# Even-odd token order kept to the store, 64-row tiles for the pair units and low-rank products, and totals moved by small transfers, in a fused recurrence and MLP kernel

## The chip, the cores and the metric

The kernel runs on one core of a Trainium2 chip. The metric is device time in microseconds (us). Three timed runs of the kernel before gave 163.08, 163.26 and 163.46 us, a median of 163.26. One further execution was profiled. The engines are TensorE (PE: matrix products, with PEld its weight loads), VectorE (DVE), ScalarE (ACT), GpSimd (POOL), and SyncE (SP), whose queue issues most transfers.

## What is computed

A gated linear recurrence on 4 batches, 8 heads, 768 tokens and head size 48, and then a mixer with a low-rank product over tokens and an MLP over channels:

```
for t in range(S):
    state = alpha[:, :, t, :, None] * state + einsum('bhd,bhe->bhde', k[:, :, t], v[:, :, t])
    y[:, :, t] = einsum('bhd,bhde->bhe', q[:, :, t], state)
x  = y with its heads side by side           # 4 x 768 x 384
h  = xt @ U @ V                              # xt: x transposed; U is 768 x 32, V is 32 x 768
u  = x + h transposed
out = u + maximum(u @ w_ch1, 0) @ w_ch2      # 384 -> 1536 -> 384
```

## The kernel before

**Chunks and pair units.** Each batch is cut into six chunks of 128 tokens. Inside a chunk the recurrence is a masked product: with cumulative sums of log(alpha) from a triangular product (lines 415 to 417 and 590), the kernel forms `rk = k * exp(-sum)` and `rq = q * exp(sum)`, transposes both (459, 632), takes scores (486, 653), masks them on DVE into `pm` (497, 663), and adds what the state brings in (560, 710) to the masked scores times v (567, 712). The state for the next chunk is the state product of rk and v (518, 676) plus the old state, scaled by the chunk's total decay `tot`.

Batches 2 and 3 go chunk by chunk (`stage_gla`). Batches 0 and 1 are "paired" (`stage_pair`): a unit holds 256 tokens of four heads, and a partition holds two neighbouring tokens, so that each row of a load is twice as long. Partitions 0 to 63 belong to the unit's first chunk, 64 to 127 to its second. To keep the two chunks apart, v is written into a tile `rw` with zeros where the other chunk's columns are, so one product of all 128 rows serves both. The transposed q is put back into natural token order when it is copied out of PSUM, which is a strided copy; from there on x is in natural order.

**Mixer.** `stage_mix` multiplies x by U in 32-column tiles of PE (line 727), which leaves four partial sums below one another; V is held four times below itself in `vm_sb`, so that the next product adds the four. Batch 0 builds the transposed u directly (746, 749). Batches 1 to 3 make u per chunk by a 128-row product with `vm_sb` (758) and an addition on DVE (759), and transpose it (774). Then come the first MLP product (801) with its Relu (811 on ACT, 813 on DVE), the second (831), a final addition (843) and the store of 128 rows (848) through SP.

**Order.** Every step is an entry of a plan. A fixed text, `TABLE`, lists all entries in one order, with a letter where an engine is chosen (A is ACT, V is DVE, G is POOL), and `Plan.run` issues them in it. So the order on every engine is written out, and buffers (36 `io` tiles for loads, 8 PSUM banks) are assigned by the plan's own estimates. Filler products that compute nothing (line 317) stand in the first 28 us. The loads wait on SP in the order of the table; SP also waits there for buffers to come free. In batch 3 the transposes of rk and rq are transfers issued by ACT (623), not PE products.

The totals of `stage_gla` come from four one-column products per chunk (592), then two exponentials on ACT (605):

```
nc.scalar.activation(tot()[:, i : 2 * HP : 2, 0], cb()[:, DM : DM + HP], AF.Exp, bias=offb[:, i : i + 1])
```

Of the kernel before, what the change touches and what calls it, by code (L numbers as in the profile page):

```python
# [159 lines left out]
69 65 61 201 157 179 63 64 62 160 204 162 165V 73 66 67 71 77 159A 161 164G 158G 167 182 169V 184 163 206 183 207 224 205 75 166 173 70 168V 186V 174  # L160
187V 170 227 229 175 188 209V 189 68 191A 232G 228 247 171 211 190V 176 172 192 194 234 250 78 208G 230 213A 180A 251 236A 185 210 181G 212V 195 177 81
214 254G 193 178V 3 256 268 252 253 196 215 74 271 72 79 197 76 4 231G 82 83 80 273 199 233 203A 202G 235A 84 198 258V 216 217 255G 272 218 226G 219
274 225A 237 85 93 6 257 5 259A 222 220 240 25 29 27 89 15 17 13 19 23 21 87 33 94 35 86 31 238 239 200A 275G 223A 95 90 221 241 260 276V 242 277 249G
248G 279A 278 2 270G 243 245 261 263 244 262 47 92 280A 264 91 97 37 43 269A 281 265 284 39 41 51 49 101 88 45 285 266 96 0 1 8 30G 28G 283 282 286 388
246A 432 391 435 267V 287 298 18G 11 9 16G 14G 288V 394 7A 289 105 57 59 53 55 290 438 437 436 10A 12V 102 291A 100 103 20G 295 292 304 301 98 293 294V
24G 22G 307 296 299 302 308 297V 305 26A 410 99 306V 303V 413 300A 326 322 107 309A 350 336 416 393 392 337V 310 414 396G 334 324 325A 415 311V 327V
335V 351V 323V 34G 32G 104 106 109 108 110 344 342 320 340 346 338 318 321A 36A 343V 395V 319A 314 398 330 341A 345A 315A 339V 439V 417V 400V 440G 356
354 412G 117 111 357V 355V 397 352 441 328 331A 347A 443V 419 442 316 411A 418G 353V 329V 444V 420 332 455 399A 333A 317A 426 348 312 421V 422V 40A
349A 38G 44G 42G 427 458 313V 428 423 429G 390G 46G 401 445 460 459 461 48A 52A 425 446 424 402 368 358 363 433G 434G 389G 50A 478 430 481 482 483 484
54G 60G 58A 499 369 447 431V 403 373 359 404 364 448 405 406 407V 449 450V 485V 408 502 56A 503 456A 409V 486V 365 370 451 371 487 462G 463V 488 504  # L170
457A 507G 360 471 489A 490A 505 465 467A 464 361 366 479A 480A 113 367 119 118 466V 472 374 491 473G 506G 468 492 375 509 494 453 469 470 511A 112 508
474 452G 378 495 618 475G 620 476 510A 376 501A 496G 621 454V 512 493 500G 515 624G 379 514 497 516 517G 513 626 623 657 622 625V 477A 129 362 114 115
659 518 662 498A 519A 627 380 629A 520 521A 637 660 628V 630 381 632 383 661 663G 664G 619G 522 524 133 121 523 525 530 384 536 534 528 531 529 537 535
526 385 527A 532 116 120 124 125 127 141 123 122 134 533V 126 665 131 372 137 135 639 666 668V 633 538 539V 634 640 641 540 642 562 548 558 542 541A
563V 643G 644G 572 646 549V 559V 717 648V 631 667V 573A 645 544 582 556 677 647A 545A 557A 649 832 669 130 128 386 583V 671 566 568 670 651 650 554 719
546 584 567A 543A 721 720 555V 697 658A 585V 586 679 547V 587V 569V 578 681 722 638G 834 652 574 635 653 575V 836 835 680 636A 682 837 387 153 655 560
550 580 684V 656V 654V 552 699 683G 553V 551A 867 701 838G 704G 570 686 685 564 579V 581V 571V 565V 702 700 678A 561A 672 703V 687V 724V 593 588 706
705 692 594 595 673 598 589 675 145 132 674V 693 707V 596 708V 839V 676V 840 688A 849 709 689 711 710 691 690 723G 851 599 725 727A 576 698G 726 600
590 712 854 577A 869 841 728A 852 718A 591 694V 872 870 613 614 729 713 731 730 138 149 382 377 143 136 142 885 921 853 871 714G 147 139 615 603 887
715 732 695 601 716V 696V 604 842 733A 889 734 923 608 735A 855G 874G 616 844 843 738 748 873G 833G 744 903 888 925 924 926 742 609 749 743 745 602 592  # L180
140 146 155 154 750 751 739 892G 610 736 746 605 752 737 850G 890 875 876 747V 753V 740 845 847 905 846 794 796 741V 797V 606 856G 891G 927G 778 768
774 848A 857 611 795V 894 858 908 893 906 760 780 764 862 152 150 144 761V 148 151 612 156 617 775V 781V 765V 863 769V 788 782 800 790 798 784 791V
779V 785V 772 758 759V 789A 907 799A 773A 801A 754 755V 756 757V 877 859 895 860 861 878 896 904A 783A 776 762 928G 864G 807 770 766 929 930 868G 909G
886G 910G 763V 767V 771V 911 802 865 912 880 803 916 808 897 777V 881 882G 879 809 898 804 812 883 813 899 900V 810 805 931 913 917 932 884A 866A 914
933 915 918G 786 792 901 827 811 806 922G 793A 902A 787A 822 934 919 920A 823 824 935V 936 828 937A 829 938 940 946 825 939 947 941 817 814 944 826 597
607 945 818 942 948 949V 943A 950 819 820 951 956 966 968 952 830 953 815 962 974 954 960 975V 970 963V 955V 976 982 994 969V 961V 995V 971A 967V 1000
992 988 993A 977A 957A 978 986 964 987V 1001V 980 958 989V 981V 959A 984 1002 990 996 983A 965A 1003A 985V 991V 997A 998 999A 972 1014 1024 1015 1004
1025 1026 1019 1020 1027 979V 973V 1021 1005 1009 1010 831 816 1028 1022 1006 1016 1007 1011 1023 821 1008 1017 1029 1012 1030 1032 1018 1013 1031 1033
1034
# [3 lines left out]
def mm(*cols):  # L193
    return sum(max(c / 2.4 + 2.5, 25.0) for c in cols)
# [3 lines left out]
def kernel(  # L198
# [12 lines left out]
    nc = tc.nc  # L211
# [20 lines left out]
    TRD = {(3, c) for c in range(NC)}  # L232
# [5 lines left out]
    u_in = const.tile([128, NC, R], FP32, name="u_in")  # L238
    v_in = const.tile([R, S], FP32, name="v_in")
# [9 lines left out]
    mask2 = const.tile([C, 2, 2 * C], BF16, name="mask2")  # L249
    for x in (filler, tri, ident, mask2, blocks):  # L250
# [6 lines left out]
        out=mask2, in_=mask2, compare_op=ALU.is_gt, fill=1.0, base=0, pattern=[[1, 2], [-1, 2 * C]], channel_multiplier=2  # L257
# [26 lines left out]
    nc.vector.tensor_copy(maskp[0:64, 0], mask2[0:64, :, 0:C])  # L284
    nc.vector.tensor_copy(maskp[64:128, 0], mask2[64:128, :, C : 2 * C])
    rv2_s = slots("rw", 4, [C, 2, HP, 2, D], BF16)
    for x in rv2_s:
        nc.vector.memset(x, 0.0)
    maskc = const.tile([C, 1, C], BF16, name="maskc")
    P.add({"POOL": 250}, lambda e: nc.gpsimd.tensor_copy(maskc[:, 0, :], ut_ones), w=["maskc"])  # L290
    sel = const.tile([R, 4, R], BF16, name="sel")
# [8 lines left out]
    tots = Pool(slots("tot", 4, [128, HP * 2, 1], FP32))  # L300
    qts = Pool(slots("qt", 4, [128, HP, C], BF16))
# [31 lines left out]
    def small():  # L333
        P.add({"SP": 450.0}, lambda e: nc.sync.dma_start(u_in, moe_U.rearrange("(c p) r -> p c r", p=128)), w=["u_in"])
        P.add({"SP": 500.0}, lambda e: nc.sync.dma_start(v_in, moe_V), w=["v_in"])
        P.add({"POOL": 300, "ACT": 280}, lambda e: copy(e, u_sb, u_in), r=["u_in"], w=["u"])
        P.add({"POOL": 800}, lambda e: nc.gpsimd.tensor_copy(v_bf, v_in), r=["v_in"], w=["v_bf"])
        for i in range(2):
            vb = Buf(bank)
            sl = slice(i * TW, (i + 1) * TW)  # L340
            P.add({"PE": mm(TW)}, lambda e, vb=vb, sl=sl: nc.tensor.matmul(vb()[:, 0:TW], lhsT=sel.rearrange("r a b -> r (a b)"), rhs=v_bf[:, sl], start=True, stop=True), r=["v_bf"] + [("sel", g) for g in range(4)], w=[vb], mode="V")
            P.add({"DVE": 470, "ACT": 390}, lambda e, vb=vb, sl=sl: copy(e, vm_sb[:, sl], vb()[:, 0:TW]), r=[vb], w=[("vm", i)])

    def weight(dst, src, key, engs):
        t = Buf(io)
        P.add({"SP": 590.0}, lambda e: nc.sync.dma_start(flat(t), src), w=[t])
        P.add(engs, lambda e: copy(e, dst, flat(t)), r=[t], w=[key])
# [4 lines left out]
    def weights1():  # L352
        for g in range(4):
            cs = slice(g * DM, (g + 1) * DM)
            for ct in range(NCT):
                weight(w1_sb[:, ct, cs], moe_w_ch1[ct * 128 : (ct + 1) * 128, cs], ("w1", g, ct), {"POOL": 485, "ACT": 435})

    def weights2():
        for jt in range(NJ):
            weight(w2_sb[:, jt, :], moe_w_ch2[jt * 128 : (jt + 1) * 128, :], ("w2", jt), {"POOL": 485, "ACT": 435})  # L360
# [24 lines left out]
    def xk(b, xb, c):  # L385
        return [(xb, c, 0), (xb, c, 1)] if b in PAIR else [(xb, c)]

    def stage_pair(b, u, sprev, xb):
# [12 lines left out]
        rv = Buf(rv2s)  # L401
# [5 lines left out]
        for c in range(2):  # L407
            P.add({"POOL": 480, "ACT": 420}, lambda e, c=c: f_rv(e, c), r=[vt], w=[(rv, c)])
# [494 lines left out]
```

## Time and profile before

| | |
|---|---|
| median of three runs | 163.26 us |
| profiled execution, whole | 164.47 us |
| its span | 162.7 us |
| PE, DVE, ACT, POOL busy | 95%, 77%, 52%, 35% |
| mean granted PE clock | 0.998 |
| transfers | 30.37 MB, mean 187 GB/s |

The span is what the profiler saw, from the first instruction to the last; the whole adds what lies around it. Busy shares are means over stages. PE's products are pipelined: the duration shown for one is its latency, and consecutive ones start closer together than that. In a merged timeline row, `x8` after a form says that eight such products follow each other, and the second number is the time from the first's start to the last's end. DMA in the slices is the mean busy share of 16 transfer engines.

### The profile page before, as it was taken

The page shows a single profiled execution, that of the slowest core. Times are in us where ns is not written, and L with a number is a line of the kernel's source. Part 1 is how long each engine was busy: PE and PEld are TensorE (multiplying, and loading weights), DVE is VectorE, ACT ScalarE, POOL GpSimd, SP SyncE. Part 2 cuts the span into 40 slices and gives each one's busy share as a digit, 9 for nine tenths or more (in the row PEclk, how much of TensorE's full clock was granted, in tenths as well). Part 3 has the DMA queues.
Part 4 walks back from the last instruction along what each step waited for, and adds up shares of the span by engine and source line. Part 5 has one row for each costly group of instructions (what it writes and reads, how often), then busy time and mean ns, then how long its engine had stood idle before and what let it go on. Part 6 is the DMA issues. An engine that isn't in the chain of part 4 may idle for free.

```text
span 162.7 us, 4458 instructions
## 1 busy us (share of the span) xinstructions
PE 154.3 (95%) x1683; PEld 102.4 (63%) x1683; DVE 125.8 (77%) x274; ACT 85.4 (52%) x218; POOL 57.7 (35%) x92
## 2 busy tenths in 40 slices
PE   7789999999999899999999999999899999999993
PEld 2356787667776676766666666766466656666662
DVE  6478996689969996979999888988978557961441
ACT  5479899557885778468982386307102411153000
POOL 3037985756264172550092056634413000000000
PEclk9999999999999999999999999999999999999999
DMA  5999999999999998998997898989982040200134
GB/s 124 271 279 302 250 277 285 326 316 330 355 253 248 207 209 185 186 202 168 216 246 64 198 204 209 218 135 189 218 108 99 0 144 7 97 0 4 48 145 145
DMA packets 89701, 30.37 MB, mean 187 GB/s; under 512 B 83376, under 2 KB 89648, under 8 KB 89680
## 3 DMA queue, kind: packets, MB, share of 16 engines
q1 hardware_dynamic: 83152, 28.52, 71.1%
q10 hardware_dynamic: 6528, 1.57, 7.4%
q8 instruction: 13, 0.21, 0.6%
q14 instruction: 8, 0.07, 0.1%
HBM read 23.79 MB, written 4.72 MB: 175 GB/s over the span
## 4 chain that ended last, share of the span: by engine, by line
PE 84%; DVE 6%; ACT 3%; DMA 3%; issue 1%; SPq 1%; DVEq 0%; ACTq 0%
PE ps L801 29%; PE ps L831 27%; PE ps L459 3%; DMA io<-in_alpha_dram 3%; PE ps L653 2%; PE ps L567 2%; PE ps L774 2%; DVE rq L446 2%; PE ps L486 2%; PE ps L758 2%; PE ps L632 2%; PE ps L518 1%; PE ps L712 1%; PE ps L590 1%; DVE st L531 1%
## 5 line engine op out<-in xcount | busy, mean ns | idle before, releaser
L831 PE MATMUL ps<-w_sb,h1t 128*128 128x384 bf16 (+2 forms) x300 | 53.1, 319 | 0.0
L801 PE MATMUL ps<-uT,w_sb 128*128 128x384 bf16 x288 | 50.9, 326 | 0.0
L801 PEld LDWEIGHTS <-w_sb 128*128 128x128 bf16 x288 | 26.8, 98 | 16.2 <-DVE uT L326 0.2
L831 PEld LDWEIGHTS <-h1t 128*128 128x128 bf16 x300 | 27.2, 98 | 15.2 <-issue 0.3
L813 DVE TENSOR_SCALAR h1t<-ps 128x384 bf16<-128x384 f32 x59 | 30.0, 551 | 6.4 <-PE ps L801 6.3
L811 ACT ACTIVATE h1t<-ps 128x384 bf16<-128x384 f32 x37 | 16.8, 500 | 16.7 <-PE ps L801 16.5
L843 DVE TENSOR_TENSOR ou<-ub,ps 128x384 f32<-128x384 bf16 (+2 forms) x19 | 9.9, 529 | 10.5 <-PE ps L831 10.3
L612 POOL TENSOR_TENSOR rk<-io,ai 128x384 bf16<-128x384 f32 x11 | 10.7, 977 | 16.7 <-ACT ai L600 11.2
L497 DVE TENSOR_TENSOR pm<-ps,maskp 128x512 bf16<-128x512 f32 x24 | 15.7, 684 | 0.3 <-PE ps L486 0.2
L663 DVE TENSOR_TENSOR pm<-ps,maskc 128x512 bf16<-128x512 f32 x24 | 15.2, 684 | 0.7 <-PE ps L653 0.6
L324 ACT CAST xb<-ps 128x384 bf16<-128x384 f32 x13 | 5.9, 480 | 14.2 <-PE ps L712 14.2
L759 DVE TENSOR_TENSOR ub<-xb,ps 128x384 bf16<-128x384 bf16 x18 | 9.0, 550 | 2.5 <-PE ps L758 2.5
L687 POOL TENSOR_TENSOR st<-sm,tot 128x384 bf16<-128x384 f32 x4 | 3.3, 828 | 18.6 <-DVE sm L699 18.6
L328 POOL CAST w_sb<-io 128x384 bf16<-128x384 f32 x16 | 7.9, 505 | 5.4 <-DMA io<-in_moe_w_ch_dram 5.2
L446 POOL TENSOR_TENSOR rk<-io,ai 128x384 bf16<-128x384 f32 x7 | 6.4, 912 | 9.1 <-ACT ai L431 6.3
L324 ACT COPY qt<-ps 128x512 bf16<-128x512 bf16 x11 | 7.7, 700 | 3.2 <-PE ps L459 1.9
L612 POOL TENSOR_TENSOR rq<-io,aa 128x384 bf16<-128x384 f32 x8 | 7.3, 914 | 2.7 <-issue 1.6
L400 ACT ACTIVATE lt<-io 128x384 bf16<-128x384 f32 x12 | 6.3, 530 | 2.9 <-DMA io<-in_alpha_dram 2.9
L317 PE MATMUL ps<-filler 128*128 128x512 bf16 x17 | 6.5, 510 | 1.2 <-DVE filler L251 1.2
L326 DVE CAST xb<-ps 128x384 bf16<-128x384 f32 x11 | 6.1, 554 | 1.8 <-PE ps L712 1.5
L446 POOL TENSOR_TENSOR rq<-io,aa 128x384 bf16<-128x384 f32 x6 | 5.9, 981 | 4.2 <-ACT aa L432 3.9
L605 ACT ACTIVATE tot<-ps,offb 128x4 f32<-128x4 f32 x24 | 4.9, 274 | 4.7 <-PE ps L801 4.5
(124 smaller groups left out, 266.2 us busy)
## 6 DMA issues: line engine op xcount, KB each, us to landing
io<-in_alpha_dram SPq DMA_DIRECT2D x24, 192.0 KB, 4.1
io<-in_q_dram SPq DMA_DIRECT2D x24, 192.0 KB, 4.3
io<-in_v_dram SPq DMA_DIRECT2D x24, 192.0 KB, 4.1
io<-in_k_dram SPq DMA_DIRECT2D x24, 192.0 KB, 4.2
io<-in_moe_w_ch_dram SPq DMA_DIRECT2D x24, 192.0 KB, 4.4
out_dram<-ou SPq DMA_DIRECT2D x23, 192.0 KB, 2.3
out_dram<-ou SPq DMA_DIRECT2D x1, 128.0 KB, 1.7
v_in<-in_moe_V_dram SPq DMA_DIRECT2D x1, 96.0 KB, 3.5
```

Of the source, the lines that this page charges most:

```text
L324: nc.scalar.copy(dst, src)
L328: nc.gpsimd.tensor_copy(dst, src)
L446: eng.tensor_tensor(jh(dst()[:, :, 0:D]), raw(a), jh(x()), op=ALU.mult)
L497: nc.vector.tensor_tensor(dst, s2, maskp.to_broadcast([C, 2, 2, C]), op=ALU.mult)
L612: eng.tensor_tensor(dst()[:, :, 0:D], a(), x(), op=ALU.mult)
L663: nc.vector.tensor_tensor(pm()[:, :, par, :], s2, maskc.to_broadcast([C, HP, C]), op=ALU.mult)
L759: P.add({"DVE": 465}, lambda e, c=c, hb=hb: nc.vector.tensor_tensor(ub()[:, c, :], xb()[:, c, :], hb()[:, 0:DM], op=ALU.add), r=[hb] + xk( ...
L801: nc.tensor.matmul(hb()[:, 0:TW], lhsT=w1_sb[:, ct, jt * 128 : (jt + 1) * 128], rhs=uT()[:, ct, tt * TW : (tt + 1) * TW], start=(ct == 0), ...
L811: nc.scalar.activation(dst, hb()[:, 0:TW], AF.Relu)
L813: nc.vector.tensor_scalar_max(dst, hb()[:, 0:TW], 0.0)
L831: nc.tensor.matmul(hb()[:, 0 : hi - lo], lhsT=h1()[:, jt, c * C : (c + 1) * C], rhs=w2_sb[:, jt, lo:hi], start=(jt == 0), stop=(jt == NJ - ...
L843: nc.vector.tensor_tensor(ou()[:, lo:hi], base()[:, c, lo:hi], hb()[:, 0 : hi - lo], op=ALU.add)
```

## The change

1. **Token order.** In batches 0 and 1 x stays in the order in which the loads bring it: in each chunk first the 64 even tokens, then the 64 odd. The transposes of q are written so that its copy out of PSUM is plain. U and V get copies in that order (`up_sb`, `vp_sb`) for batches 0 and 1, and `u_sb`, `vm_sb` are made from them by a product with a permutation and by two copies on POOL. The output rows of a chunk go out in two transfers of 64 rows.
2. **Pair units in 64-row tiles** (`HALF`). v is cast once into a plain tile. The state products and the products of masked scores with v are issued per chunk on 64 rows of PE, into two PSUM banks; two such products can be in PE at once. The part from the state is issued after them, untiled, and the output leaves in two copies of 192 columns instead of one of 384.
3. **Low-rank products in 64-row tiles** (`ROWS`, batches 1 to 3). The U products are made twice, so that each half of the 128 rows holds the whole sum; then two chunks' low-rank products run on the two halves.
4. **Late totals** (`TOTD`, batches 2 and 3). The one-column products go. ACT takes the exponential of the last 32 rows of the sums, and two transfers of 48 pieces of 16 bytes move the last row into `tot`, for five of six chunks; the sixth needs none.
5. **Engines and order.** v and weight casts may go to DVE, and `TABLE` is another order throughout, which begins with a load of q, then three of alpha.

New lines: state products 570, output products in the chunk 617, from the state 629, permutation 360, U products 869, low-rank 903, totals 705 and 708, stores in halves 1009. Cut to its core:

```diff
+        for j in range(2):
+            P.add({"SP": 330.0}, lambda e, j=j: nc.sync.dma_start(u_in[64 * j : 64 * j + 64], moe_U.rearrange("(c m j) r -> j m c r", c=NC, j=2)[j]), w=[("u_in", j)])
...
-        for c in range(2):
-            P.add({"POOL": 480, "ACT": 420}, lambda e, c=c: f_rv(e, c), r=[vt], w=[(rv, c)])
+        if apart:
+            P.add({"POOL": 480, "ACT": 420, "DVE": 340}, lambda e: copy(e, flat(rv), flat(vt)), r=[vt], w=[(rv, 0), (rv, 1)], port=True)
...
+                if apart:
+                    for c in range(nch):
+                        r = slice(64 * c, 64 * c + 64)
+                        for m in parts:
+                            nc.tensor.matmul(
+                                db[c]()[m, a * 2 * D : (a + 1) * 2 * D],
+                                lhsT=rk()[r, HP * j + 2 * a : HP * j + 2 * a + 2, :].rearrange("t h w -> t (h w)")[:, m],
+                                rhs=raw(rv)[r, j, 2 * a : 2 * a + 2, :],
+                                start=(n == 0), stop=(n == 3 and not onpe), skip_group_check=True,
+                            )
+                    continue
...
+            def f_yn(e):
+                for h in range(HP):
+                    for j in range(2):
+                        for c in range(2):
+                            r = slice(64 * c, 64 * c + 64)
+                            for m in parts:
+                                nc.tensor.matmul(
+                                    yb[c]()[m, h * D : (h + 1) * D], lhsT=pm()[r, (h // 2) * 2 + j, h % 2, m], rhs=raw(rv)[r, j, h, :],
+                                    start=(h == 0 and j == 0), stop=(before[c] is None and h == HP - 1 and j == 1), skip_group_check=True,
+                                )
...
+        def f_end(e):
+            nc.scalar.activation(end()[C - 32 : C].rearrange("t i d p -> t p i d"), cb()[C - 32 : C, 0:DM].rearrange("t (p i d) -> t p i d", i=2, d=D), AF.Exp)
+
+        def f_move(e, i):
+            nc.sync.dma_start(tot()[64 * i : 64 * i + D, HP * i : HP * i + HP, 0], end()[C - 1 : C, i].rearrange("t d p -> t (d p)"))
...
+                for gg in (g % 2, g % 2 + 2) if twice else (g,):
+                    nc.tensor.matmul(
+                        xu()[32 * gg : 32 * gg + R, 0:DM], lhsT=us[:, c, :], rhs=xb()[:, c, :],
+                        start=(c < (2 if twice else 4)), stop=(c + (2 if twice else 4) >= NC), skip_group_check=True,
+                    )
...
+        def f_low(e, c):
+            for i in range(2):
+                r = slice(64 * i, 64 * i + 64)
+                nc.tensor.matmul(hbs[c + i]()[:, 0:DM], lhsT=vs[r, (c + i) * C : (c + i + 1) * C], rhs=utx()[r], start=True, stop=True)
...
+                def f_store(e, z=z):
+                    nc.sync.dma_start(out[b, c * C : (c + 1) * C, :].rearrange("(m j) x -> j m x", j=2)[z], ou()[64 * z : 64 * z + 64, :])
```

## The prediction

> **What bounds the kernel now.** I read the page's busy shares and its 40 slices first, then the list of waits of TensorE (PE), then the PE groups by form, then PE's timeline where small products meet long ones, then the landings of the transfers.
>
> ```profile
> span 162.7 us, 4458 instructions
> PE 154.3 (95%) x1683; PEld 102.4 (63%) x1683; DVE 125.8 (77%) x274; ACT 85.4 (52%) x218; POOL 57.7 (35%) x92
> PE   7789999999999899999999999999899999999993
> DVE  6478996689969996979999888988978557961441
> PEclk9999999999999999999999999999999999999999
> DMA  5999999999999998998997898989982040200134
> ```
> PE is busy in nearly every slice at full granted clock. VectorE (DVE) runs at 0.9 in the first stage and in the middle; the DMA engines are full until slice 30 (about 120 us).
>
> ```profile
> PE ps L459 <- DVE rq L446: 1.2, 2, 0.9
> PE ps L653 <- DVE pm L663: 0.8, 1, 0.8
> 115.77 0.23 PEld L653 LDWEIGHTS <-kt 48*128 48x128 bf16 x8 [0.96 <-DMA kt<-rk]
> ```
> Waits of PE, and a weight-load row. Comparing each start with the one before, I find 2.4 us of PE stall from 28.5 us to the end, nearly all in two places: 1.1 at 52.3 us, behind a run of DVE work, and 1.0 at 115 us, where weights wait for a transposing transfer. Before 28.5 us, from the first real product (6.65 us) on, there are about 3 us of gaps. So the time is PE's work plus a few waits, and the first term is a count.
>
> ```profile
> L567 PE MATMUL ps<-rw,pm 128*128 128x96 bf16 x96 | 6.0, 206 | 0.0
> L758 PE MATMUL ps<-utx,vm_sb 128*128 128x384 bf16 x18 | 4.4, 326 | 0.0
> L518 PE MATMUL ps<-rw,rk 128*128 128x192 bf16 x32 | 4.0, 246 | 0.4 <-ACT rw L324 0.4
> L592 PE MATMUL ps<-ones,lt 128*128 128x1 bf16 x48 | 2.9, 164 | 0.0
> L727 PE MATMUL ps<-xb,u_sb 128*32 128x384 bf16 x24 | 2.0, 333 | 0.0
> L518 PE MATMUL ps<-rw,rk 128*128 128x96 bf16 x16 | 1.4, 207 | 0.0
> ```
> The groups that the change replaces. The mean is a latency; what counts is the step from start to start:
>
> ```profile
> 64.33 0.40 PE L653 MATMUL ps<-qt,kt 48*128 48x128 bf16 x8
> 64.66 0.82 PE L831 MATMUL ps<-w_sb,h1t 128*128 128x384 bf16 x4
> 65.32 0.65 PE L758 MATMUL ps<-utx,vm_sb 128*128 128x384 bf16 x3
> 79.99 0.36 PE L712 MATMUL ps<-rv,pm 128*128 128x48 bf16 x8
> 80.20 0.33 PE L710 MATMUL ps<-st,qt 128*128 128x96 bf16 x4
> 80.36 0.36 PE L712 MATMUL ps<-rv,pm 128*128 128x48 bf16 x8
> ```
> Four of 384 columns take 0.66 us (64.66 to 65.32): 162 ns each. Eight of 48 columns take 0.21 (25 ns each), four of 96 take 0.16 (42 each). L653 has pairs in 64-row tiles: single starts in the trace are 3 to 4 ns apart inside a pair, for the weight loads too, and 56 from pair to pair, so two 128-column products cost what one does. Going into and out of a tiled shape costs 95 ns each time (L831 to L653: 258 ns instead of 162; L653 back: 148 instead of 56).
>
> **PE's work, part by part.** Removed: totals of batches 2 and 3 (L592), 48 x 25 = 1.20 us. State products (L518), 32 x 82 + 16 x 42 = 3.30. Output products in the chunk (L567), 96 x 42.5 = 4.08. Low-rank products (L758), 18 x 162 = 2.92. U products (L727), four batches of two rounds of 162 = 1.30. Sum 12.80.
>
> Added: state products in 64-row tiles, 32 pairs and 16 singles of 96 columns, 48 x 42 = 2.02. Output products, 192 of 48 columns in 96 pairs: no row shows a pair that short. Two ends: 25 ns for a pair, as for one product in L712 (2.40 us), or 50, if two short ones follow each other (4.80). I take 25, since L653's loads and products start together, and in 16 products of 64x64 tiles (L486) a product starts every 14 ns. Low-rank in pairs, 9 x 162 = 1.46. U products twice over in batches 1 to 3, 2 + 9 rounds = 1.79. The reordering of U, 0.08. Sum 7.75. Net -5.05.
>
> Against it stand changes of tile shape. In PE's order there are 39 before and 73 after (state and output products now are tiled and lie between untiled ones): 34 x 0.095 = +3.23. **PE's work: -1.8 us.**
>
> Here a rule weighs against the change. The Trainium skill, TensorEngine Tiling (Array Packing), section Instruction Overhead, says that each matmul carries about 60 cycles, and warns not to split by tiling when a dimension is already short. Taken per instruction (25 ns at 2.4 GHz), the 192 output products would cost an estimated 4.8 us and PE's work would grow by 0.6 us. The 14 ns steps of L486 contradict that reading across tiles; no row here shows it at 48 columns.
>
> **First stage (to the first MLP product, 28.92 us).** The first load issued is now a q; the first PE step needs the second load, not the third. These landed at 4.0 and 6.05 us, so PE starts up to 2 us earlier. Later the stage is held by DVE and ScalarE (ACT). Per pair unit the change removes one of two v casts of 0.5 us (ACT or POOL), makes the q eviction plain (0.73 to 0.42 on DVE, 0.74 to 0.58 on ACT) and splits the output eviction (0.55 into two of about 0.35). DVE's order from its first two masks (about 12.2 us by these steps) to the last one holds 10 masks of 0.61 from start to start, 9 state scalings of 0.27, four multiplies of 0.47 and smaller copies, 11.3 us in all; with 0.8 for waits on data that land until about 21 us (the last v is issued one place later) I place the last mask at 24.3 us (24.7 before) and the first MLP product at 28.1. Ends: 27.3, if all three engines' relief shows, and 29.4, if the late v or POOL's multiplies hold it. Of the 0.8, 0.4 is one cumulative-sum group moved behind it, in the sum already. **-0.4 us** (-1.2 to +0.9).
>
> **Later stages.** DVE loses four Relu evictions, four to six multiplies and the strided copies, and gains three weight casts: about 8 us less, so the stall at 52.3 us should shrink (-0.7; ends -1.1 and +0.5, since pair units now use two more banks). The two stores per chunk in batches 0 and 1 move the same rows: 12 more issues of about 0.36 us on the SP queue, nothing on PE.
>
> The late totals: ACT's two operations of 0.27 become one on 32 rows; nearest row 0.49, so nothing. Then SP waits for it and issues two transfers of 48 pieces, 20 in all. The smallest transfer shown (128 KB out) lands in 1.7 us, the median load in about 4. In PE's order at least 13 us of work lie between a chunk's cumulative sum and the state product that uses the total, so landing is hidden. What stands behind them on SP is loads, and stores of batches 0 and 1, and this is not free: the last v landed at 117.7 us, the last transposed q at 124.28, and the score product needing it started at 124.68. Price: 20 + 12 issues of 0.36 are 11.5 us on SP, against 30 us in which SP waited from 50 to 120 us. I take +1.1 for batch 3 (0 to +5).
>
> The skill's page DMA: Bandwidth & Descriptors, Rules for kernel authors, says that transfers under 64 KB are mostly overhead and should be merged, and gives a fixed 2 us. At an estimated 2 us each the 13 us of cover still hold; only queueing would hurt.
>
> **Sum.** -1.8 - 0.4 - 0.7 + 1.1 = -1.8. The profiled execution took 164.47 us (span 162.7 and 1.8 around it), 1.2 above the median of the three timed runs, 163.26. I subtract from the median: **161.4 us**; the profiled execution should show a span near 160.9.
>
> **Rivals.**
> - *Batch 3's transfers set the end.* If the last transposed tile lands when it did, only what follows it counts: by the same steps PE had 34.7 us of work left after the last score group began, and has 33.7 now. Then -1.0: 162.3. For it: DMA at 0.95 to 1.03 from 90 to 120 us and the 0.4 us margin. Against it: just one PE wait of about 1 us there.
> - *Slower: the SP queue.* The same place, but loads and with them the transposes slip by d behind the totals' waits and issues. Time 162.3 + d: it decides from d = 1.0 us. A quarter of the 11.5 us gives 165.2. Against it: the queue's waits leave room.
> - *Pairs of 48 columns do not overlap.* Each costs 50 ns: +2.4, 163.8.
> - *More than forecast.* First stage 27.3 and no stall added in batch 3: -1.8 - 1.2 - 0.7 + 0.1, 159.7 to 160.2.
>
> **How the numbers follow.** Chances: forecast 0.48 (own range 160.5 to 162.2), batch 3 0.16, SP 0.11, no overlap 0.09, more 0.16. About 0.2% (0.33 us) is what a measurement here tells from no change. Faster: 0.48 + 0.16 + 0.13 of batch 3 = 0.77; within: 0.03 of batch 3 and 0.02 of no overlap; slower: 0.11 + 0.07. The range 159.7 to 163.9 leaves out most of the SP case and the edge of the best one.
>
> **What would show it.** Right: output products of 64 rows at 12 to 13 ns from start to start; tile changes still 95 ns; first MLP product near 28 us; PE stalls after it of about 3 us. Wrong: 25 ns steps there; loads of batch 3 landing after 119 us with PE waiting for a transposed tile; or PE stalls in the units of batch 1, where pair units now follow each other with few long products between.

## The result and the profile after

The changed kernel takes **170.35 us** (median of 4 runs, 169.84 to 174.44) against 163.17 us for the kernel before (4 runs, 162.05 to 163.46). The ratio is 1.0445, with a 95% interval of 1.0389 to 1.0501: about 7.3 us slower, where 1.8 us less was forecast. Single executions differ, in part by what PE's clock did: in some it is halved for a stretch of some 3.4 us, the profiled one has two of these, and the ratios in this document leave out executions that took over 1.5% more than the fastest of their kernel.

The page of the changed kernel, the lines that answer to those shown of before:

```profile
span 172.6 us, 4662 instructions
PE 157.6 (91%) x1782; PEld 100.8 (58%) x1782; DVE 119.5 (69%) x265; ACT 90.5 (52%) x213; POOL 60.3 (35%) x96
PE   7795999999999999999999946999998699999993
DVE  6069896558887999565977445599987589547142
PEclk9999699999999999999999998799999999999999
DMA  5999999799999219797957878979989443000154
```

PE's slices, which were 8 or 9 from the first stage to the end, now have holes at slices 23, 24, 30 and 31, counted from 0 (99 to 108 and 129 to 138 us). The transfer engines, full until slice 30 before, fall to 0.1 or 0.2 at slices 13 and 14 (56 to 65 us), stay at 0.5 to 0.8 in several of the ten slices that follow, and go on until slice 33. So the transfers became later without moving more at a time.

The rows that replace the groups of before, and the new transfers (the page's part 6 gives the size of one and its time to landing):

```profile
L617 PE MATMUL ps<-rv,pm 64*128 64x48 bf16 x192 | 4.8, 182 | 0.1
L570 PE MATMUL ps<-rv,rk 64*128 64x96 bf16 x80 | 4.4, 211 | 0.3 <-ACT aa L696 0.2
L903 PE MATMUL ps<-utx,vm_sb 64*128 64x384 bf16 x12 | 1.9, 332 | 1.3 <-DVE ou L995 1.2
L705 ACT ACTIVATE end<-ps 32x384 f32<-32x384 f32 x10 | 8.4, 862 | 0.2
out_dram<-ou SPq DMA_DIRECT2D x24, 96.0 KB, 2.4
totz<-end SPq DMA_DIRECT2D x20, 0.8 KB, 3.0
```

PE's part is as forecast: the starts of the 48-column products (L617) are 3 to 4 ns apart inside a pair and 21 to 22 ns from pair to pair, so a pair takes 25 ns, and a change of tile shape still costs 95 ns. Rows of the second look show it: eight pairs take 0.21 us, from 48.87 to 49.08.

```profile
48.87 0.37 PE L617 MATMUL ps<-rv,pm 64*128 64x48 bf16 x16
49.08 0.33 PE L570 MATMUL ps<-rv,rk 64*128 64x96 bf16 x8
```

The exponential of the last rows takes 0.86 us, not the 0.49 of the row it was priced by. A total of 0.8 KB needs 3.0 us to land.

PE's waits show where the time went:

```profile
PE ps L849 <- POOL st L793: 2.6, 1, 2.6
PE ps L507 <- DVE rq L492: 2.1, 2, 1.6
PE ps L849 <- DVE sm L805: 1.4, 1, 1.4
PE ps L903 <- DVE ou L995: 1.2, 1, 1.2
```

L849 multiplies by the state, which waits for a total. L903 waits for PSUM that an output addition frees, which waits for a store. Both end at SP's queue. Only the second line (L507, in the first stage) is of another kind.

**A ledger from two second looks.** Both kernels were profiled once more, unchanged.

> The kernel before, unchanged, profiled a second time. The forecast took 0.7 us for the stall at 52.3 us and counted on the one at 115 us, both read in one profiled execution that took 1.2 us more than the median. If these stalls belong to the kernel: 1.0 us at both places again, and PE stalls of about 2.4 us after 28.5 us. If they belonged to that execution: 1 to 1.5 us of stalls in all, with the span nearer to 161.4.

> The changed kernel, unchanged, profiled a second time, since its first profile has two stretches of half clock and took 4 us more than its median. Expected if SP's issues are the cause: the last load issued near 134 us again, about 20 us later than before, PE stalls of 8 to 11 us after the first MLP product, most of them between 69 and 137 us; the first MLP product at 28 to 30.5 us, according to how long the q scaling at 13.3 us takes (0.6 or over 2 us).

Second looks: before 163.58 us, span 161.8; changed 170.24 us, span 168.5. Between these spans, +6.7 us, I put PE's time together from product starts (a stall is a step longer than the products' own by over 15 ns):

- first MLP product: 29.00 to 28.24 us, -0.8
- PE's work from there to the last product, without stalls: 128.3 to 127.1, -1.2
- stalls after 28.5 us: 1.5 to 10.2, +8.7

The sum is +6.7. The 10.2 us hold one stretch at half clock, behind the wait of 2.4 us that is shown below; its row (length, busy us of PE, PEld, DVE, ACT and POOL with counts, granted clock, share of transfers, GB/s) puts some 1.5 us of the 10.2 down to slower steps, half of its length less a part in which PE stood:

```profile
99.40:102.80 3.40, 3.02 (x25) 1.49 (x28) 2.29 (x5) 2.44 (x5) 0.33 (x1) 0.50 0.86 179
```

The expectations were met in part: the span of before came at 161.8, not 161.4, and the last load of the changed kernel at 130.6, not near 134. Of the two stalls read in the first profile of before, the one at 52.3 us is 0.1 in the second look and so not in every execution; the one at 114 us is there in both (1.0 and 1.1).

### The profile page after: what moved, and what is told of

Same layout as the page of the kernel before. It is cut to its first block, busy times and chain, and to the rows that moved or that the text cites. A ratio compares the mean times of both kernels' runs of the same rounds, so it can differ in the third digit from the quotient of the medians.

```text
span 172.6 us, 4662 instructions
## 1 busy us (share of the span) xinstructions
PE 157.6 (91%) x1782; PEld 100.8 (58%) x1782; DVE 119.5 (69%) x265; ACT 90.5 (52%) x213; POOL 60.3 (35%) x96
## 2 busy tenths in 40 slices
DMA packets 91190, 30.40 MB, mean 176 GB/s; under 512 B 84864, under 2 KB 91136, under 8 KB 91168
## 4 chain that ended last, share of the span: by engine, by line
PE 55%; DMA 19%; ACT 3%; issue 2%; POOL 2%; DVE 2%; SPq 1%; DVEq 0%; POOLq 0%; ACTq 0%
PE ps L953 22%; PE ps L983 19%; DMA qt<-rq 5%; DMA kt<-rk 3%; DMA out_dram<-ou 3%; DMA io<-in_alpha_dram 3%; DMA totz<-end 2%; DMA io<-in_q_dram 2%; PE ps L507 2%; DMA io<-in_v_dram 2%; PE ps L531 2%; PE ps L926 1%; POOL rk L722 1%; ACT end L705 1%; PE ps L570 1%
## 5 line engine op out<-in xcount | busy, mean ns | idle before, releaser
L983 PE MATMUL ps<-w_sb,h1t 128*128 128x384 bf16 (+2 forms) x300 | 55.0, 326 | 0.4 <-ACT aa L696 0.3
L965 DVE TENSOR_SCALAR h1t<-ps 128x384 bf16<-128x384 f32 x55 | 28.4, 552 | 11.5 <-PE ps L953 9.1
L963 ACT ACTIVATE h1t<-ps 128x384 bf16<-128x384 f32 x41 | 19.2, 503 | 22.7 <-PE ps L953 16.8
L722 POOL TENSOR_TENSOR rq<-io,aa 128x384 bf16<-128x384 f32 x10 | 9.1, 916 | 12.9 <-ACT h1t L963 8.0
L338 ACT CAST xb<-ps 128x192 bf16<-128x192 f32 (+1 forms) x24 | 8.6, 377 | 2.9 <-PE ps L629 2.2
L342 POOL CAST rv<-io 128x384 bf16<-128x384 f32 x15 | 7.5, 505 | 7.3 <-DMA io<-in_v_dram 6.4
L492 POOL TENSOR_TENSOR rq<-io,aa 128x384 bf16<-128x384 f32 x8 | 7.3, 913 | 7.4 <-ACT aa L478 7.0
L478 ACT ACTIVATE aa<-ps 128x384 bf16<-128x384 f32 x12 | 6.1, 508 | 5.8 <-DVE sm L604 4.0
L695 ACT ACTIVATE ai<-ps 128x384 bf16<-128x384 f32 x12 | 5.8, 492 | 5.8 <-PE ps L685 5.8
L705 ACT ACTIVATE end<-ps 32x384 f32<-32x384 f32 x10 | 8.4, 862 | 0.2
L338 ACT COPY kt<-ps 128x512 bf16<-128x512 bf16 x10 | 6.0, 596 | 3.6 <-PE ps L507 3.6
```

The source lines that it names most:

```text
L338: nc.scalar.copy(dst, src)
L342: nc.gpsimd.tensor_copy(dst, src)
L492: eng.tensor_tensor(jh(dst()[:, :, 0:D]), raw(a), jh(x()), op=ALU.mult)
L705: nc.scalar.activation(end()[C - 32 : C].rearrange("t i d p -> t p i d"), cb()[C - 32 : C, 0:DM].rearrange("t (p i d) -> t p i d", i=2, d= ...
L722: eng.tensor_tensor(dst()[:, :, 0:D], a(), x(), op=ALU.mult)
L963: nc.scalar.activation(dst, hb()[:, 0:TW], AF.Relu)
```

## The experiments

**What was asked.** Theory A: the 32 extra transfers (20 totals, 12 half stores) on SP's queue delay the loads of batches 2 and 3. Theory B: the new order of work, PSUM or the other engines cause the stalls.

*Totals on PE.*

```
-        sums = c < NC - 1 and not moved
+        sums = c < NC - 1
...
-            P.add({"ACT": 400}, f_end, r=[cb], w=[end])
+            P.add({"ACT": 200}, f_tot, r=[cb], w=[(tot, 0), (tot, 1)])
```

> The changed kernel with one part undone: in batches 2 and 3 the totals come from four one-column products on PE again, as before, and the 20 small transfers and their exponentials are gone. The half stores of batches 0 and 1 stay. PE gets 40 one-column products back, 40 x 25 ns = 1.0 us. Theory A (the late totals' transfers slow the stream of loads on SP, so the tiles of batches 2 and 3 come late): the stalls of PE after 28.5 us fall from 12 to about 4 us and the last transposed tile lands before 127 us; time 162 to 165. Theory B (the transfers are beside the point; the stalls come from the new order of the work, PSUM banks or the other engines): the stalls stay, and with PE's 1.0 us the time is 170 to 171.5.

*Dummy transfers.* The same, with a pair of transfers per chunk that nobody waits for:

```
+ nc.sync.dma_start(totz_s[n // 2 % 4][64 * z : 64 * z + D, 0:HP, 0], fill_s[0][C - 1 : C, z].rearrange("t d p -> t (d p)"))
```

> Totals on PE as in the run with the totals on PE, but 20 transfers of the same size and form stand at the same places of SP's queue. They read a constant tile and write a tile that nobody reads, so SP waits for no exponential there and no engine waits for their landing. It tells apart what a total costs. If it is the waits (SP standing until ScalarE has made the total, the state scaling standing until the total has landed): time as without them, 162 to 165. If it is the transfers themselves (SP's 0.6 us per issue, the place among the transfers in flight that each holds for 3 us): 167 to 170.5, near the changed kernel. If the transfers are beside the point (theory B): 170 to 171.5, here and in the run without them.

*Whole stores.*

```
-  for z in range(2): nc.sync.dma_start(out[...].rearrange("(m j) x -> j m x", j=2)[z], ou()[64 * z : 64 * z + 64, :])
+  nc.sync.dma_start(out[b, c * C : (c + 1) * C, :], ou())
```

> The changed kernel with one store of 128 rows per chunk in batches 0 and 1 in place of two of 64; the late totals by small transfers stay. The rows of these two batches come out in the even-odd order, so this leaves out the reordering. 12 transfers fewer. If every extra transfer costs the same (12 of 32 of a loss of some 8.5 us against the forecast): 3.2 us less than the changed kernel, about 167. If only the totals' small transfers cost: 169.5 to 170.5. Theory B: 169.5 to 170.5 as well.

*Both undone.*

> Totals on PE and whole stores together: none of the 32 extra transfers is left, all that the change does on PE, VectorE and in the order of the work stays (the rows of batches 0 and 1 come out in the even-odd order). Theory A: the forecast without its +1.1 us for batch 3 and with 1.0 us of PE work back, 161 to 162.5. Theory B: 169 to 171.5. If it lies between, near 165, both have a share.

| kernel | time, us | ratio to before (95%) | last load issued, us | stalls over 0.1 us after the first MLP product, to 1 or 2 us |
|---|---|---|---|---|
| before, second look | 163.58 | | 113.3 | 1.5 |
| changed, second look | 170.24 | 1.0445 (first runs) | 130.6 | 8.1 |
| totals on PE | 164.41 | 1.0047 (1.0010 to 1.0085) | 120.0 | 1.1 |
| dummies on SP | 168.25 | 1.0280 (1.0208 to 1.0353) | 128.2 | 6.2 |
| whole stores | 167.44 | 1.0224 (1.0144 to 1.0303) | 128.0 | 4.9 |
| both undone | 163.12 | 0.9964 (0.9926 to 1.0002) | 114.4 | 0.6 |

Theory B falls. Both undone takes 7.2 us off the changed kernel, though it stays 0.6 us above the range expected for it, and its interval just takes in no change from before. With both undone, the new order, the new tiles and the new sharing of engines are all still there, and all that PE waits for from 32 us on is one line:

```profile
PE ps L507 <- DVE rq L492: 0.4, 1, 0.4
```

The moment at which the last load is issued shows how it works. The last load's row, in SP's timelines of before and of the changed kernel (second looks), and of the run with totals on PE, in this order:

```profile
113.34 0.37 SPq L377 DMA_DIRECT2D io<-in_v_dram  x1
```
```profile
130.55 0.58 SPq L418 DMA_DIRECT2D io<-in_v_dram  x1
```
```profile
119.98 0.54 SPq L418 DMA_DIRECT2D io<-in_v_dram  x1
```

Between 50 us and the last load SP issues 56 transfers before and 85 after. The last load is 17.2 us later, 0.59 us for each of the 29 more. In SP's rows, issues fill 48.8 us of this stretch before and 62.4 after, so 13.6 us are issues and the rest is longer gaps between them. A transfer of 0.8 KB takes SP no less time than one of 96 KB: the totals take 0.52 to 1.53 us (median 0.65), the half stores 0.49 to 1.53 (median 0.60).

The dummies cost 3.8 us more than none (168.25 to 164.41) although SP never waits for an exponential there and nobody waits for their landing. So the larger part of a total's price is its place on SP's queue. Totals that are awaited cost 2.1 us more than dummies (170.35 to 168.25; 2.7 by the ratios), although PE is spared 1.0 us of products: some 3 us for the waits and for ACT's longer exponential together, which no run parts. SP's longest wait before the last load is at the first total, in its timeline of the second look:

```profile
54.97 0.55 SPq L1009 DMA_DIRECT2D out_dram<-ou  x1
59.69 0.58 SPq L708 DMA_DIRECT2D totz<-end  x1
```

For 4.2 us SP issues nothing, until that total's exponential ends at 59.7. From 54 to 60 us the transfer engines are 0.37 busy, against 0.87 before and 0.77 with dummies. A later total made PE wait, in order of time:

```profile
93.52 1.47 SPq L708 DMA_DIRECT2D totz<-end  x2
95.03 0.58 SPq L418 DMA_DIRECT2D io<-in_alpha_dram  x1
95.66 0.78 SPq L708 DMA_DIRECT2D totz<-end  x1
98.90 0.83 POOL L793 TENSOR_TENSOR st<-sm,totz 128x384 bf16<-128x384 f32 x1 [3.10 <-DMA totz<-end]
99.78 0.48 PE L849 MATMUL ps<-st,qt 128*128 128x96 bf16 x4 [2.42 <-POOL st L793]
```

That total's exponential had ended at 89.7 us. Its second transfer was issued at 95.66, behind other transfers on SP, landed at 98.74, and PE had waited 2.4 us. Over the ten chunks, 7.4 to 22.2 us pass from the end of the exponential to the landing (median 10.4).

**Which resource of the queue.** In the traces SP's and ACT's transfers together use 8 completion semaphores, and SP's rows show it waiting for the transfer that used the same one last. These are the 8 places in flight. The dummies were issued from other queues to part SP's time from these places and from the transfer engines (an edit of one word, `nc.sync` to `nc.scalar` or `nc.gpsimd`).

> The 20 dummy transfers are issued by ScalarE's queue in place of SP's, at the same places of the plan; everything else as in the run with dummies on SP. They still share the 8 places in flight with SP's transfers. If what they cost is SP's time (0.6 us of issue each, between loads that SP issues back to back): 164 to 165.5, as with totals on PE and no dummies, unless ScalarE's own 12 us of issuing delay PE. If it is the places in flight: 167 to 168.5, as with dummies on SP.

> The 20 dummy transfers are issued by GpSimd's queue: they take neither SP's time nor one of the 8 places in flight of SP's and ScalarE's transfers; only the work of the DMA engines and of memory is left. SP's time or the places in flight: 164 to 165.5. The DMA engines: 167 to 168.5. GpSimd's own work is delayed; it is busy for 61 of 166 us, so that should cost under 0.5 us.

From ACT the last load is issued at 122.9 us, from GpSimd at 120.4, with no dummies at 120.0 and with dummies on SP at 128.2. So some two thirds of the delay of the loads is SP's own time, the rest goes with the places in flight, and the transfer engines add nearly nothing. The split is rough: it rests on one execution of each, and the one with dummies on SP had its first MLP product over 3 us earlier than the others. With the dummies on ACT, SP's waits show the places held by them:

```profile
SPq L421 <- DMA totz<-end: 5.5, 5, 2.9
```

But ACT's queue was no way out: 170.33 us (ratio 1.0438, 1.0358 to 1.0517), outside both forecasts. From the first MLP product to the end the profiled executions take 138.1 us with the dummies on ACT and on SP alike, 134.0 on GpSimd and 132.4 with none. By these profiles the 2 us by which ACT is worse than SP lie in the first stage, which is treated below. ACT's issues take 0.60 us each, and ACT stands while its transfers wait, with Relu evictions behind them. Waits of ACT and of PE in that run:

```profile
ACT h1t L966 <- DMA qt<-rq: 6.9, 1, 6.9
ACT h1t L966 <- DMA out_dram<-ou: 6.8, 1, 6.8
```
```profile
PE ps L956 <- ACT h1t L966: 2.6, 3, 1.3
```

With the dummies on GpSimd the median is 166.41 us of four runs. Three of these have a mean PE clock of 0.979 to 0.990, in the profiled one by the hole in the first stage that is treated below; the one at full clock took 163.24. A ratio is not to be had from one run; its profile has 2.3 us of stalls after the first MLP product, where dummies on SP had 6.2.

**Can the transfers go to GpSimd?**

> The changed kernel whole, with all 32 extra transfers, but issued elsewhere: the late totals and the second half store of each chunk go to GpSimd's queue, and the q scaling of the first stage goes one instruction earlier. SP then issues as many transfers as before; the output is the reference's. If SP's time is the cause: the last load is issued at 114 to 118 us, stalls after the first MLP product under 3 us, time 160.8 to 162.5, so at or below the kernel before. If the transfers themselves cost (DMA engines, landing of the totals): 165 to 169. A loss of its own could come from GpSimd standing for a total or an output with multiplies behind it: up to 2 us.

```
-            nc.sync.dma_start(tot()[64 * i : 64 * i + D, ...
+            nc.gpsimd.dma_start(tot()[64 * i : 64 * i + D, ...
...
-                    nc.sync.dma_start(out[...][z], ...
+                    (nc.gpsimd if z else nc.sync).dma_start(out[...][z], ...
```

172.50 us, ratio 1.0574 (1.0527 to 1.0620): worse than the changed kernel, and a clear miss. Real totals, unlike dummies, make the issuing engine wait. Its waits, GpSimd's and then PE's:

```profile
POOL totz L708 <- ACT end L705: 14.2, 4, 5.8
```
```profile
PE ps L570 <- POOL rv L342: 2.7, 1, 2.7
PE ps L849 <- POOL st L793: 2.0, 1, 2.0
```

GpSimd stood 14.2 us for exponentials, with casts of v and multiplies behind, and the last load is issued at 122.8 us all the same. SP's own waits from 50 us to that load show why:

```profile
SPq L1009 <- DVE ou L995: 7.5, 2, 5.4
SPq L1009 <- DVE qt L340: 6.6, 1, 6.6
```

SP stands with the first half stores (L1009) for VectorE's late outputs, up to 6 us at a time, and the loads stand behind. In the changed kernel's second look the waits of L1009 are 3.3 us. That VectorE is late because GpSimd is, I read from the order of the work; no run shows that part by itself.

> Totals on PE, the second half store of each chunk on GpSimd's queue, the q scaling one instruction earlier; the output is the reference's. SP issues as many transfers as before and GpSimd 12. If SP's time is the cause: as with both undone and the multiply earlier, 162 to 163. If the half stores cost by being two (their landing, the DMA engines): 163.5 to 164.5, as with totals on PE and half stores on SP.

165.29 us over all ten executions; the ratio of 1.0064 (1.0010 to 1.0118) leaves out five of them. The last load is back at 114.9 us, as with both undone, but the time is not, as neither forecast had it: PE's largest wait, 1.6 us, is for ACT (the Relu of L963). Why it comes there I have not tested.

**The price on the kernel before.**

> The kernel before with one thing added: 20 small transfers that nobody waits for on SP's queue, each pair at the place of a chunk's totals in batches 2 and 3. Nothing else of the change is in it. If a transfer on SP's queue costs the loads behind it 0.4 to 0.7 us whatever the kernel around it: the last load is issued at 121 to 127 us instead of 113.3, PE waits for transposed tiles and inputs of batch 3, time 166 to 170. If the price needs the new order of the changed kernel: 163 to 164.5.

> The kernel before with the stores of batches 0 and 1 split in two transfers of 64 rows each, 12 transfers more on SP's queue; the output is the reference's. At 0.46 us each (the last load 5.5 us later in the run with totals on PE) the last load is issued at 117 to 120 us, time 164 to 166. If the half stores cost only in the changed kernel: 163 to 163.8.

Dummies alone: 168.44 us, ratio 1.0284 (1.0202 to 1.0367), last load at 120.7 us. Half stores alone: 165.66 us, 1.0126 (1.0049 to 1.0203), last load at 118.7. That is 4.6 and 2.1 us, with nothing else of the change. The loads are later by 7.4 us behind 19 more transfers (0.39 each) and by 5.3 behind 9 more (0.59). PE's waits with the dummies and then with the half stores:

```profile
PE ps L660 <- DVE ou L850: 2.0, 1, 2.0
PE ps L808 <- ACT h1t L818: 1.7, 2, 0.8
```
```profile
PE ps L653 <- DMA kt<-rk: 1.2, 1, 1.2
```

So the price belongs to the queue, not to the changed kernel's order. The two prices and the gain of all the rest (-0.6, both undone) give 6.1 of the 7.3 us. What is special to real totals, some 3 us less the 1.0 us of spared products, is more than enough for the rest; the parts overlap and do not add up exactly.

**The first stage.** In the first profile of the changed kernel one VectorE multiply takes four times its usual time, and a hole in PE's work and a half clock follow. VectorE and GpSimd there, and then four stretches with columns: length, busy us of PE, PEld, DVE, ACT, POOL with counts, granted clock, share of transfers, GB/s:

```profile
13.29 2.33 DVE L492 TENSOR_TENSOR rq<-io,aa 128x384 bf16<-128x384 f32 x1
```
```profile
13.44 0.90 POOL L492 TENSOR_TENSOR rk<-io,ai 128x384 bf16<-128x384 f32 x1
14.31 0.90 POOL L492 TENSOR_TENSOR rq<-io,aa 128x384 bf16<-128x384 f32 x1
```
```profile
14.00:16.00 2.00, 0.37 (x6) 0.28 (x5) 2.00 (x2) 1.34 (x4) 1.21 (x2) 1.00 0.99 259
16.00:18.00 2.00, 1.46 (x33) 1.01 (x31) 2.00 (x6) 0.31 (x1) 1.41 (x2) 1.00 1.05 269
18.00:20.00 2.00, 1.99 (x34) 1.47 (x35) 1.55 (x5) 0.93 (x2) 0.00 (x0) 0.56 0.96 249
20.00:22.00 2.00, 2.00 (x34) 1.70 (x33) 1.61 (x4) 1.69 (x5) 1.78 (x3) 0.59 0.99 252
```

The multiply ends 0.4 us after GpSimd's second one. The Trainium skill, SBUF — State Buffer, section "SBUF: two separate sides", says that VectorE and GpSimd share one pair of ports as an exclusive lock, which a VectorE operation with two inputs in SBUF needs against a GpSimd operation that reads SBUF, and that the loser blocks for the whole instruction; the 2.33 us agree with standing through both. In the second look the same multiply takes 0.86, the hole is gone and the first MLP product comes at 28.24 us instead of 30.40.

Theory C was that this ate the gain. The edit moves one entry in the table:

```
- ... 240V 220V 181 74 72 ... 73 87 241V 187G ...
+ ... 240V 220V 241V 181 74 72 ... 73 87 187G ...
```

> Both undone as before (totals on PE, whole stores, so the rows of batches 0 and 1 come out in the even-odd order), and one VectorE multiply of the first stage, the q scaling at about 13.5 us that took 1.48 us there (2.33 in the profile of the changed kernel, 0.57 in the run with dummy transfers), goes one instruction earlier in VectorE's order, ahead of a state scaling, so that it meets a short GpSimd cast and not GpSimd's run of copies and two multiplies. Theory C (that multiply stands behind GpSimd's instructions, and the hole of 1 to 2 us that it leaves in PE's work at 14 us, with the half clock after it, ate the gain of the first stage): the multiply takes 0.6 to 0.9 us, the first MLP product starts at 27.6 to 28.6 us instead of 29.9, the time is 161 to 162. Rival (the hole is covered by later waits): 162.7 to 163.5 as without it.

> The run with totals on PE, with the same multiply one instruction earlier. Half stores stay, the output is the reference's. Theory C: 162 to 163.3 (1 to 2 us below the 164.4 of that run), at or a little below the kernel before. Rival: 164 to 165.

The multiply takes 0.55 us in both profiles, and the clock stays at 0.998 or above in all ten runs of each kernel. In the four profiles with the multiply moved (these two and the two with real transfers on GpSimd) it takes 0.55 to 0.89 us; in the eight without, 0.57 and 0.86 in two and 1.48 to 2.33 in six. That fits GpSimd's instructions making it long. But the time does not follow: 162.40 us, ratio 0.9963 (0.9936 to 0.9990), the same as without the move, and its first MLP product comes at 29.2 us, not 28. With totals on PE the ratio is 1.0075 (1.0046 to 1.0104) and the first product at 28.2, a miss as well. Theory C falls as a cause of the median. The collision goes with a wider spread of single executions: ten span 3.0 us without the move and 1.0 with it, 2.3 and 1.6 with totals on PE. No version here that stores the rows in natural order beats the kernel before.

## Why the prediction was wrong

- **Late totals and half stores on SP (+1.1 taken, 0 to +5 kept): the step that failed.** 32 issues of 0.36 us were set against 30 us in which SP waited. The term, taken at +1.1, measured 7.2 us (changed kernel against both undone), or 8.2 with the 1.0 us of products that the late totals spare PE. An issue took some 0.6 us in the busy stretch, and the 30 us were no room: a wait in that list runs from the end of one issue to the release of the next, and part of it lies inside that next issue's row. In the second look of before the list gives 25.7 us from 50 us to the last load, but SP stands between its rows for only 14.7 of 63.1 us. The new issues did not fill these gaps: the ones over 0.2 us are 10.5 us in 6 places there, and 13.3 us in 9 places in the changed kernel. The loads of batch 3 came 17 us later, and PE stalled 8.7 us more, half clock included. The test written down, loads of batch 3 landing after 119 us with PE waiting, came out as said: the last landed at 133.4 us in the second look (116.9 before).
- **"Landing is hidden" behind 13 us of PE work: wrong.** 3.0 us of landing would have been; the total's place in SP's queue made it 7.4 to 22.2 from exponential to landing. The forecast's own sentence, that only queueing would hurt, named the thing and did not price it.
- **ACT's exponential "so nothing":** 0.86 us each, 0.37 more than the row it was priced by, 3.7 us over ten. ACT is busy for 90 us instead of 85. What it cost PE alone was not tried.
- **PE's work (-1.8): right in mechanism, a little large.** -1.2 after the first MLP product. What the count took from before that product, where other engines set the time, should not have stood beside the first stage's own term.
- **Pairs of 48 columns:** 25 ns per pair, as assumed. The rule of the Trainium skill, TensorEngine Tiling (Array Packing), section Instruction Overhead, read per instruction as in the prediction, would have given an estimated 50 per pair; the trace contradicts that reading.
- **First stage (-0.4, first MLP product at 28.1):** 28.24 in the second look, 30.40 in the first. It was right in single executions in which the multiply was short, but with the multiply moved it still came between 28.2 and 29.2.
- **Stall at 52.3 us (-0.7): half an accident.** It is 0.1 us in the second look of before, and 1.1 in three other profiles (the first of before, and before with dummies and with half stores). The forecast took gains from the stalls of one execution that was 1.2 us above the median, and subtracted them from the median.
- **Rivals.** "Slower: the SP queue" is what happened, with the right place and mechanism, but a price of a quarter of 11.5 us and a chance of 0.11. With the transfers undone and the totals on PE, the rest of the change gains 0.6 us (the interval reaches 0), where the forecast's other terms with the totals' 1.0 us put back make 1.9.

## What to carry to other kernels

Price an added transfer first by its place on the queue that issues it: where loads are issued back to back, each new one, of 0.8 KB or of 96 KB, delayed the loads behind it by 0.4 to 0.6 us here, and a queue's summed waits are not slack that new issues will fill. A transfer that must wait for a result held up what stood behind it on SP and on GpSimd, so moving it to another queue moved the wait. And read a stall that a forecast wants to remove in two executions before taking it.

## What was not expected of the hardware

An issue took the issuing engine's time, and no less for a small transfer: for 0.8 KB 0.50 us on GpSimd, 0.60 on ACT, 0.52 and more on SP; a 192 KB store late in the changed kernel, with nothing around it, takes 0.33. The Trainium skill, DMA: Bandwidth & Descriptors, section "Anatomy of one DMA — SWDGE (gpsimd) path", puts a sequencer's dispatch at some 50 ns for GpSimd's path; the rows of GpSimd's issues last 504 ns, ten times as long. For the price of an issue the measured row decides; whether it holds more than the dispatch, no run here shows.

In the first stage the same multiply took between 0.55 and 2.33 us in profiles of nearly the same program; in two profiles of one and the same program, 2.33 and 0.86.
